# Two token blocks as one unit: first-layer matmuls of 256 rows in place of 128, and the weight traffic that goes with it

## The chip, the cores and the metric

The kernel runs on one core of a Trainium2 chip. The time is the device time of one execution in microseconds, the median of several runs. Five engines work side by side: TensorE (PE in the profile, its weight loads PEld), VectorE (DVE), ScalarE (ACT), GpSimd (POOL) and SyncE (SP), which issues nearly all transfers to 16 DMA engines. All arrays are 32-bit floats.

## The reference

Eight batches of 576 tokens go through a linear attention, a Fourier mix and a two-layer network:

```python
num = einsum('bhsm,bhmd->bhsd', phi(q), einsum('bhsm,bhsd->bhmd', phi(k), v))
x   = num / den                          # to (8, 576, 512)
u   = x + real(fft(fft(x, axis=1), axis=2))
un  = (u - mean(u)) / sqrt(var(u) + 1e-06)
out = u + maximum(un @ w_ch1, 0) @ w_ch2 # w_ch1 512 x 2048, w_ch2 2048 x 512
```

The change concerns the last line alone, and of the 4608 tokens in it those that go in blocks.

## The kernel before

**Two phases.** The first, up to about 421 us, does the attention, the Fourier mix and four plain rows of 128 tokens (`plain_of`, L1136), whose results `rest` (L1198) adds to u and stores. It ends in `listing.run` at L1415. The second (L1436) takes the other 4096 tokens in eight blocks of 512 (`NTB`, `TB`) and multiplies with two levels of Strassen-Winograd: a product of two matrices is cut into 2 x 2 parts and made of seven smaller products of sums of the parts, and each of these is cut again.

**First layer.** `first_of(j, i)` (L1466) makes outer product i (1 to 7) of block j. It consists of seven leaves (`leaf`, L1480), one for each inner product. A leaf is four matmuls, each with a stationary tile of 128 x 128 of a weight sum (left factor) and 128 rows (tokens) of a token sum: L1495. The rows are walked as 4 pieces of 32, a step that comes from the transposition in blocks of 32 (`by_blocks`, L1021). Each leaf's 128 x 512 result lies in a PSUM bank; VectorE and ScalarE copy it out, add it up (`save`, `added`, `moved`) and put it into four cells of `hid` (C11, C12, C21, C22). In block 0, products 2 to 7 are done with one level only (`single`, L1226), by matmuls of 256 rows at L1646.

**Weights of the first layer.** `w1` (128 x 4 x 2048) stays in SBUF, as do the outer sums `so[5]`, `so[6]`, `so[3]`, and `w1s`, the inner sums of product 1. Inner leaves 1, 2, 4 and 7 are read there in place. For the other products the inner sums 5, 6 and 3 are made once during block 0 (`w1_inner`, L1734), stored to DRAM (`w1l`, 18 stores of 256 KB) and loaded again for every block from 1 on, 18 loads a block (L1789).

**Second layer.** `product_of(j, i, cells)` (L1833) makes product i of block j: sums of hidden cells (`left_sums` L1687, `add_up` L1848), seven leaves of four matmuls (L1892) and the results' sums in `part` and `ur`. All its 49 weight tiles a block (`w2l`, 256 KB each) are loaded for every block (L1798). These and the first layer's loads share a ring of 12 buffers (`wl`, `NWL`).

**Tokens.** For block j, `norm_of` (L1061) loads 128 rows of u, normalizes them on ScalarE and POOL, transposes on VectorE (L1024) and stores to DRAM (`turned`, L1032). `fetched` (L1034) loads the tokens of half a block in four transfers of 128 KB (L1040). `block_norms` (L1270) then makes the outer token sums `tt` (L1290) and `token_sums` the inner ones (L1257), in `rx`.

**Order of the work.** Nothing is left to a scheduler: `manual_schedule` is on, and `Listing.run` (L233) merges generators of `Step`s into one order for each engine. A step names its engine, its planned time, what it waits for (`after`), the buffers it takes and gives, and a due time, which for block j, layer and product is

```python
    def due(j, layer, i):
        order_ = order(j) if layer else ORDER1 if j else ORDER0
        return LEAF * (98 * j + 49 * layer + 7 * order_.index(i))
```

The planner takes, among steps that can start at about the same time on an engine, the one due first. The start of the second phase is given instead by two strings, `PICKS2` and `BANKS2`. Transfers are planned with a rate (`Clock.rate`, 190 in `SECOND`, L56). At most three products are in flight (`set=3`). Transfers of all kinds stand in SP's one queue in the planned order, and a step that waits there holds back those behind it.

Of the kernel before, what the change touches and what calls it, by code (L numbers as in the profile page):

```python
# [1 line left out]

# [38 lines left out]
class Clock(NamedTuple):  # L41
# [14 lines left out]
SECOND = Clock(190.0, 0.15, 0.0, 0.1, {}, {}, (PE, ACT, DVE, POOL, SP, NONE), {})  # L56
# [41 lines left out]
    "0w0w0v000u0v0x0y0y0v0y0x0x0v0y0w0z0y0u0t1z0M0u0M1K0K0u1v0Q0N0I0t0W0M0O1L1w0L1U1t0S0Q0R0u010U0S0O0G0G"  # L98
    "0P0T1u0R0s0s000S0O0N0N0T0I0P0z0L0Q0R1R0B0K1P0P0K0K0T0V0I0S0G0U0T0S0U1s0H1r0D0z0x0A1N0w0F0S0P0F0E0O1O"
    "1u0R0v0G0V0V0V0C0S1S0R0L0w0P0S1r0V0M0Q0O0u0y0R0H0L1s0U0P0E0F0M0R1r0D0W0M0#0&0u0T0$0W0M0R0J0L0C0O0V00"  # L100
    "0$0N1q0M0R0G0A0V0u0Z0A0A0Z0R0U0D0S0S0L0G0Z0H0P1Y0F0F0Z0Y1q0$0$0C0D0D0U0T0X0T0#0X0z0V0F0U0V0X0C0B0W0P"
    "0R0U0T0U0v0T0x0Y0N1P0z0u0O0z0I0T0M0N0T0K0A0N0R0x0G0W1F0X0L0I0M0I0x0G0T0U0x0R0R0x0G0I0A0R0G0O0O0E0x0M"
    "0V0U000t0E1G1t0T1L0K0B0O0E0P1L0M0u0K0G1Q0L0R1z0N0C0E0G0E0u0G0D0L1D0N0C1Q0K1O0L0S0M0y0C0T0A0B1L0t0U0U"
    "0T0G0L0R0O0E0R0K0O0M0A0J0L0E1r1z1R0z0K0C0y0y0M0O0M1t0I0A0F0D0C0J0I0E1D0L0C0s1K0H0F0J0J0w0z0I0D0E0H1E"
    "0C0J1E0F0p0M0o0L1K1H1N0M0B0O0G0C0F0J0A0J0J0N0p1G0C1B0H0N0y0E0E0I1H0y1K0G0z0B0L0H0G0N1H0M0H0M0M0M0M1E"
    "0C1J0G0B1I0B1E0y0G0u1E0F0B0D1D1E0u0F0F0y0A0z0y0G0C0J0A0p0D0G0y1G0C0F0z0p0E0u1w0A0D1w0y0y0x0z0F0t0E0B"
    "0F0E1x1v1z1D0C0A0E0E0C0z0t1z0D0C0D1C0B0D0u0x0B0r0x0C0v0A1y0v0u0v0t0t0A0u0o0s0z0A1x0y0C0z0y0A0x0D0A0t"
    "0D0E0E0E0D0A0z0y0z0B0q0s0C0A0x1r0x0z0z1t1D1D0t0s0u0v0r0t0v000u0u0q0r0A1A0x0z0A0s0z0A1q0z0x0y0A0p0v0u"
    "0x0p0p0z0x0x0y0t0w0y0r0q0v0r0q000n0t0E0r0r0n0E0F0A0A0A0G0z0F0p0x0z0L0L0x0z0y0x0H0J0o0w0G0C0G0m0x0v0E"
    "0w0z0A0v0B0x0F0G0A0D0B0I0z0z0G0C0m0E0x0y"  # L110
)
BANKS2 = (
    "5670152675637645127567567560754361752071640532471365062476735"
# [219 lines left out]
def kernel(  # L333
# [10 lines left out]
    nc = tc.nc  # L344
# [42 lines left out]
    w1 = const.tile([128, NDC, DFF], F32, name="w1")  # L387
# [633 lines left out]
    def by_blocks(j, i, pool, u, h, k):  # L1021
        yield Step(DVE, 0.69, take=("turn",), give=("u",), makes=("turn", j, i))
        w = pool.tile([P, 4, NDC, Q], F32, name="turn", tag="turn", bufs=1)
        nc.vector.transpose(  # L1024
            out=w[:].rearrange("p g d q -> p d g q"),
            in_=u[:].rearrange("p (d g q) -> p d g q", d=NDC, g=4),
        )
        if (j, h) not in turned:
            turned[j, h] = dram.tile([P, 4, 2, NDC * Q], F32, name=f"turned{j}_{h}")
        t = turned[j, h]  # L1030
        yield Step(SP, 0.55, 6.0, after=(("turn", j, i),), makes=("turned", j, i), give=("turn",), kb=165)
        nc.sync.dma_start(t[:, :, k], w[:].rearrange("p g d q -> p g (d q)"))  # L1032

    def fetched(j, h, dst):  # L1034
        yield Step(
            SP, 1.7, 3.0, after=(("turned", j, 2 * h), ("turned", j, 2 * h + 1)),
            makes=("unT", j, h), kb=330,
        )
        for g in range(4):
            nc.sync.dma_start(  # L1040
                dst[Q * g : Q * g + Q].rearrange("q (b k) d t -> q b (k d t)", k=2),
                turned[j, h][:, g].rearrange("(b q) k n -> q b (k n)", q=Q),
            )

    def normed(j, pool):
        t0 = (NPLAIN * TP + TB * j) // 128

        def paced(i):
            h, k = divmod(i, HT // 128)
            yield Step(  # L1050
                NONE,
                after=events_of(range(t0, t0 + TB // 128)) + ((("first", j - 1, (1, 1, 5, 2)[i]), "y"),),
            )
            yield from norm_of(
                j, t0 + 2 * h, i, pool, None, (h, k), ((("first", j - 1, (6, 2, 7, 3)[i]), "y"),)
            )

        for i in range(TB // 128):
            yield Fork(paced(i), LEAF * (98 * j - 60 + 8 * i))

    def norm_of(j, t, i, pool, dst, block=None, after=()):  # L1061

        yield Step(SP, 0.42, 3.0, take=("u",), kb=256)
# [134 lines left out]
    def rest(t, b, yp):  # L1198
# [6 lines left out]
        store_rows(t, ur[:])  # L1205

# [18 lines left out]

    def single(j):  # L1226

        return () if j else ORDER0[1:]
# [10 lines left out]
    def tokens(j, i, n):  # L1239

        whole = outer_tokens(j, i)
        if n in (1, 2, 3, 7):
            t, d = {1: (0, 0), 2: (0, 1), 3: (1, 1), 7: (1, 0)}[n]
            return whole[:, 4 * t : 4 * t + 4, d]
        return extra_of(j, i)[:, (5, 6, 4).index(n)]

    def extra_of(j, i):
        if i == 1:
# [10 lines left out]
    def token_sums(j):  # L1259
        if j == 1:  # L1260
            yield Step(NONE, after=tuple(("w1l", i, n) for i in twice(1) for n in (5, 6, 3)))
        for i in twice(j):
            for m, op in enumerate(inner_tokens(j, i)):
                yield Step(
                    DVE, 0.28, after=(("tt", j),), makes=("tokens", j, i) if m == 3 else None, port=True,
# [4 lines left out]
    def block_norms(j, pool):  # L1270
        t0 = (NPLAIN * TP + TB * j) // 128
        yield Step(NONE, take=("slab",) * 4, after=events_of(range(t0, t0 + TB // 128)) + ("converted",))
# [36 lines left out]


# [63 lines left out]
    GW = F2 // 2  # L1374
    w1s = const.tile([128, 4, GW], F32, name="w1s")

# [7 lines left out]
    def weights_of(j, i, n):  # L1384
# [21 lines left out]
    def pairs(start):  # L1406
# [28 lines left out]
        slab=0, u=2, turn=1, ur=3, s=6, sq=5, set=3, wl=NWL, sums=NSUM, part=4,  # L1435
    ).items()}  # L1436
    hid = late.tile([128, 4, 2, 2, 4 * P], F32, name="hid")
    so.update({i: late.tile([128, D2, F2], F32, name=f"so{i}") for i in (5, 6, 3)})
# [7 lines left out]
    def cell_of(c, f, t):  # L1446
        return hid[:, c, f, t]
# [7 lines left out]
    def add(o, l, r, op, engines=(POOL, DVE), **kw):  # L1455
        n = math.prod(o.shape[1:]) / 512
        step = Step({e: {POOL: 1.3, DVE: 0.65}[e] * n + 0.05 for e in engines}, port=True, **kw)
# [8 lines left out]
    def first_of(j, i):  # L1466
        me = ("first", j, i)
        slot, read = slot_of(j, i), READ.get(i)
        free = ((("second", j - 1, read), "read"),) if read and j else ()
        merged, final = i in WITH, i in (2, 3, 4)  # L1470
# [3 lines left out]
        def over(f, t):  # L1474

            if i == 2:
                return (("h", j, 6, f, t),) if j else ()
            return {7: (("h", j, "u4", f, t),), 4: (("h", j, "sum", f, t),)}.get(i, ())

        def leaf(n, ps, start, after=(), take=(), give=(), makes=None):  # L1480
            own = n in (5, 6, 3) and i != 1
            w = ("wx", 1) if i == 1 else ("wx", j, i, n) if own else ("so", i, n)
            token = (("tokens", j, i),) if i != 1 else (("tt", j),)
            yield Step(
                PE, 0.895, after=token + (w,) + after, take=take, give=(("wl",) if own else ()) + give,
# [7 lines left out]
            left, right = weights_of(j, i, n), tokens(j, i, n)  # L1493
            for f in range(4):
                nc.tensor.matmul(  # L1495
                    ps[:, P * f : P * f + P].rearrange("f (b q) -> f b q", q=Q),
# [8 lines left out]
        def made(f, t):  # L1505
            return ("h", j, i, f, t)

        def with_(f, t):
            return (("h", j, BEFORE[i], f, t),)
# [48 lines left out]
        def last_cell(f, t):  # L1558
            o = cell_of(C22, f, t)
            after = ("h", j, 7, f, t), ("h", j, "u4", f, t)  # L1560
            yield from add(o, o, cell_of(C21, f, t), ALU.add, after=after, makes=("h", j, "sum", f, t), bias=due(j, 0, 4) - due(j, 0, 5) - 1)
# [3 lines left out]
        def u4_cell(f, t):  # L1565
# [3 lines left out]
                after=(read, made(f, t), ("h", j, 6, f, t)), makes=("h", j, "u4", f, t),  # L1569
# [10 lines left out]
        if i in single(j):  # L1580
# [19 lines left out]
            def u4_of(f, c, b, ps):  # L1600
                read = ((("second", j - 1, READ["u4"]), "read"),) if j else tuple(
                    ("h", j, n, f, t) for n in (2, 6) for t in range(2)
                )
                yield Step(
                    DVE, 0.7, 0.1, after=read + tuple(("h", j, 6, f, t) for t in range(2)) + ((me, "half", f, c),),
# [4 lines left out]
            def whole(f):  # L1610
# [4 lines left out]
                else:  # L1615
                    here = tuple(("h", j, "u4 half", f, c) for c in range(2))
                    for t in range(2):
                        yield Step(NONE, after=here, makes=("h", j, "u4", f, t))
# [69 lines left out]

# [382 lines left out]
```

## Time and profile before

| | |
|---|---|
| median of 3 runs | 1131.79 us (1131.77 to 1135.15) |
| profiled execution | 1134.51 us, span 1132.7 us |
| TensorE | busy 1116.3 us of the span |
| VectorE, ScalarE, POOL | busy 867.6, 541.7, 428.1 us |
| DMA | 258.30 MB, mean 228 GB/s |
| first-layer matmuls of 128 rows (L1495) | about 275 ns each from start to end, pipelined |
| one-level matmuls of 256 rows (L1646) | about 379 ns each, pipelined |
| w2 loads, first-layer weight loads | 392 and 126 of 256 KB |
| granted TensorE clock | 1.00 in nearly every stretch |

The span is what the profiler saw of one execution; the device time lies around it. "Busy" counts the time in which at least one instruction of an engine runs. Since matmuls overlap, the cost of one is not its mean duration but the distance to the next, read from a run of them without gaps. In the lines of the profile an instruction group is written as line, engine, operation, output<-input; an arrow before a name at the end tells what a wait ended with.

### The profile page before, as it was taken

What the parts mean: (1) busy time and instruction counts of PE and PEld (TensorE: products, weight loads), DVE (VectorE), ACT (ScalarE), POOL (GpSimd) and SP (SyncE); (2) the same over time, 40 slices, a digit from 0 to 9 for tenths busy, and PEclk for the clock granted to TensorE, in tenths of its full rate; (3) what the DMA queues carried; (4) which work ended last, traced back from release to release, by engine and by line L of the source; (5) the groups of instructions that cost most, each with busy time, mean ns of one, the idle gap of its engine ahead of it and who ended that gap; (6) DMA issues with size and microseconds to landing.
All of it is one profiled execution on the core that took longest, in us unless ns stands there. A gap on an engine that the chain in (4) does not pass through costs nothing.

```text
span 1132.7 us, 34265 instructions
## 1 busy us (share of the span) xinstructions
PE 1116.3 (99%) x13643; PEld 1040.2 (92%) x13643; DVE 867.6 (77%) x1732; ACT 541.7 (48%) x1644; POOL 428.1 (38%) x438
## 2 busy tenths in 40 slices
PE   8999999999999999999999999999999999999998
PEld 7778888879868778999999999999999999999998
DVE  6999899987576655796787778678678678678666
ACT  7888898856535216614424424424423522522311
POOL 2443443654573214613612710710720630540361
PEclk9999999999999999999999999999999999999999
DMA  7856766565763238797797798797698698798576
GB/s 242 224 177 180 224 181 215 170 206 170 222 196 126 93 92 284 211 314 246 227 339 232 219 329 241 213 326 258 202 323 264 210 281 298 214 268 293 184 223 205
DMA packets 187966, 258.30 MB, mean 228 GB/s; under 512 B 52384, under 2 KB 83360, under 8 KB 187808
## 3 DMA queue, kind: packets, MB, share of 16 engines
q1 hardware_dynamic: 187312, 255.85, 73.1%
q8 instruction: 109, 1.79, 0.7%
q14 instruction: 49, 0.40, 0.1%
q10 hardware_dynamic: 496, 0.26, 0.1%
HBM read 212.27 MB, written 47.97 MB: 230 GB/s over the span
## 4 chain that ended last, share of the span: by engine, by line
PE 89%; DVE 4%; ACT 3%; DMA 2%; issue 1%; SPq 0%; DVEq 0%; ACTq 0%
PE banks L1892 28%; PE banks L1495 28%; PE banks L1167 5%; PE banks L658 5%; PE banks L1190 5%; PE banks L564 4%; PE banks L1646 4%; PE banks L692 3%; PE banks L739 2%; PE banks L901 2%; ACT e L618 1%; PE banks L851 1%; DMA unT<-turned 1%; DVE nmx L601 1%; PE banks L861 1%
## 5 line engine op out<-in xcount | busy, mean ns | idle before, releaser
L1892 PE MATMUL banks<-wl,sums 128*128 128x128 f32 x1792 | 218.9, 275 | 0.7 <-DVE sums L1460 0.7
L1892 PEld LDWEIGHTS banks<-wl,sums 128*128 128x128 f32 x1792 | 209.3, 192 | 1.1 <-DVE sums L1460 0.9
L618 ACT ACTIVATE e<-banks,nmx 128x128 f32<-128x128 f32 x576 | 164.3, 423 | 24.3 <-DVE nmx L601 23.7
L1460 POOL TENSOR_TENSOR hid<-hid 128x512 f32<-128x512 f32 x97 | 127.0, 1314 | 119.1 <-ACT hid L1552 66.5
L1892 PE MATMUL banks<-wl,hid 128*128 128x128 f32 x1344 | 170.6, 275 | 0.6 <-DVE part L1870 0.4
L1892 PEld LDWEIGHTS banks<-wl,hid 128*128 128x128 f32 x1344 | 160.2, 192 | 1.1 <-DVE part L1870 0.6
L601 DVE TENSOR_REDUCE nmx<-banks 128x8 f32<-128x1024 f32 (+1 forms) x96 | 89.4, 952 | 18.3 <-PE banks L658 14.2
L1495 PE MATMUL banks<-rx,wx 128*128 128x128 f32 x672 | 88.8, 275 | 0.0
L1865 ACT ACTIVATE s<-banks 128x128 f32<-128x128 f32 x112 | 30.8, 277 | 113.2 <-PE banks L1892 97.7
L1495 PEld LDWEIGHTS banks<-rx,wx 128*128 128x128 f32 x672 | 81.8, 192 | 0.0
L658 PE MATMUL banks<-om,kqT 64*64 64x128 f32 (+1 forms) x2088 | 78.7, 275 | 2.2 <-ACT kv L708 1.9
L1538 DVE TENSOR_TENSOR hid<-banks,s 128x512 f32<-128x512 f32 x72 | 49.7, 691 | 38.9 <-PE banks L1495 36.9
L658 PEld LDWEIGHTS banks<-om,kqT 64*64 64x64 f32 (+1 forms) x2088 | 64.3, 138 | 13.1 <-issue 3.6
L1870 DVE TENSOR_TENSOR part<-banks,s 128x128 f32<-128x128 f32 x112 | 32.1, 288 | 50.0 <-PE banks L1892 48.8
L1520 ACT ACTIVATE s<-banks 128x512 f32<-128x512 f32 x65 | 38.7, 596 | 59.7 <-PE banks L1495 58.6
L1167 PE MATMUL banks<-unT,w 128*128 128x128 f32 x512 | 65.4, 279 | 1.7 <-DVE qeT L578 1.7
L507 POOL TENSOR_TENSOR w<-w,raw 128x512 f32<-128x512 f32 x28 | 37.7, 1356 | 77.6 <-DVE raw L501 77.6
L1442 DVE CUSTOM_DVE_ANT_0 hid<-banks,s 128x512 f32<-128x512 f32 x63 | 43.6, 692 | 27.5 <-PE banks L1495 25.2
L1167 PEld LDWEIGHTS banks<-unT,w 128*128 128x128 f32 x512 | 60.2, 192 | 4.5 <-issue 2.3
L1460 DVE TENSOR_TENSOR hid<-hid 128x512 f32<-128x512 f32 x91 | 61.1, 712 | 3.8 <-ACT hid L1598 3.8
L1518 DVE TENSOR_TENSOR s<-banks,hid 128x512 f32<-128x512 f32 x70 | 48.4, 691 | 19.0 <-PE banks L1495 16.7
L1941 POOL TENSOR_TENSOR ur<-ur,part 128x512 f32<-128x512 f32 x21 | 26.8, 1281 | 95.4 <-ACT part L1934 91.6
(200 smaller groups left out, 2387.4 us busy)
## 6 DMA issues: line engine op xcount, KB each, us to landing
wl<-w2l SPq DMA_DIRECT2D x392, 256.0 KB
wx<-w1l SPq DMA_DIRECT2D x126, 256.0 KB
raw<-in_moe_w_ch_dram SPq DMA_DIRECT2D x32, 512.0 KB
kq<-in_k_dram SPq DMA_DIRECT2D x32, 288.0 KB
kq<-in_q_dram SPq DMA_DIRECT2D x32, 288.0 KB
vd<-in_v_dram SPq DMA_DIRECT2D x32, 288.0 KB
u<-us SPq DMA_DIRECT2D x36, 256.0 KB
ur<-us SPq DMA_DIRECT2D x36, 256.0 KB
```

The costliest lines, as they stand in the source:

```text
L564: nc.tensor.transpose(ps[:, (j - j0) * 128 : (j - j0 + 1) * 128], src(j), ident[:])
L601: nc.vector.tensor_reduce(nmx[:, :, 0:num], pps[:, :, 0 : MF * num].rearrange("p b (c m) -> p b c m", m=MF), axis=AX.X, op=ALU.max, negate ...
L618: nc.scalar.activation(out=e[:, c + (i if num == 1 else 0), :], in_=pps[:, i, MF * c : MF * c + MF], func=AF.Exp, bias=nmx[:, i, c : c + 1],)
L658: nc.tensor.matmul(pps[cols, c, MF * m : MF * m + MF], lhsT=kqT[rows, j, cols], rhs=om2[rows, :],)
L1167: nc.tensor.matmul(hp[:, 0:TP], lhsT=w1[:, dc, 128 * fc : 128 * fc + 128], rhs=unTs[key][:, dc, :], start=(dc == 0), stop=(dc == NDC - 1),)
L1190: nc.tensor.matmul(yp[:, 0:DM], lhsT=hs[fc][:, 128 * i : 128 * i + 128], rhs=w2[:, fc, :], start=(fc == 0), stop=(fc == NFC - 1),)
L1460: eng.tensor_tensor(out=o, in0=l, in1=r, op=op)
L1495: nc.tensor.matmul(ps[:, P * f : P * f + P].rearrange("f (b q) -> f b q", q=Q), lhsT=left[:, P * f : P * f + P], rhs=right, start=start an ...
L1518: nc.vector.tensor_tensor(out=s[:], in0=ps, in1=cell_of(addend, f, t), op=ALU.add)
L1538: nc.vector.tensor_tensor(out=o, in0=ps, in1=kept[saved][:], op=ALU.add)
L1646: nc.tensor.matmul(cell.rearrange("f t (b q) -> f t b q", q=Q), lhsT=w[:, d, col : col + 128], rhs=right[:, :, d].rearrange("f (t b) q -> ...
L1892: nc.tensor.matmul(ps[:, 0:128], lhsT=left[:, f], rhs=wls[j, i, n][:, f], start=start and f == 0, stop=(f == 3), skip_group_check=True,)
```

## The change

From block 2 on, two blocks (2 and 3, 4 and 5, 6 and 7) form a unit (`WIDE`, `head`, `unit`, `passes`).

- First layer: a product is done in two passes g, each with half of the weight columns (256 of 512) and the tokens of both blocks. A leaf is two matmuls of 256 rows in place of four of 128. Cells hold both blocks' hidden values; half of them lie in `hid`, half in the memory of `w1` (`spread`, `widened`, `moved`).
- Because `w1` is given up, all 49 inner weight tiles are stored to DRAM (`w1x`): the 18 as before, nine that are plain parts of w1 right behind the stores of the first three plain rows (`RAW`, in `rest`), 12 during block 0, six during block 1 and four after the first pass of unit 2's product 1 (`w1_stored`). Units load them by two half tiles a transfer. Unit 2's product 1 reads w1 and `w1s` in place.
- Second layer: product i of the first block is followed by product i of the second with the same weight tile, which is loaded once for both.
- Tokens: both blocks of a unit are fetched before it, in twice as many transfers of 64 KB, into the memory of `so[5]` and `so[6]`; token sums are of 256 tokens; norms are paced over the unit before.
- The planner's transfer rate goes from 190 to 240, with new `PICKS2` and `BANKS2`; sums of hidden cells in the last unit go to VectorE only; the last order of products holds for both blocks of the last unit.

```diff
-SECOND = Clock(190.0, ...
+SECOND = Clock(240.0, ...
...
+        for i, n in RAW[4 * t : 4 * t + 4] if t < 3 else ():
+            nc.sync.dma_start(leaf_in(i, n), weights_of(0, i, n))
+    RAW = [(i, n) for i in (1, 2, 4) for n in (1, 2, 4)]
...
+    WIDE = 2
+    def wide(j):
+        return j >= WIDE
+    def head(j):
+        return j - (j - WIDE) % 2 if wide(j) else j
+    HEADS = tuple(j for j in range(NTB) if head(j) == j)
+    def unit(j):
+        return range(j, j + 2 if wide(j) else j + 1)
+    def passes(j):
+        return range(2 if wide(j) else 1)
...
-    def weights_of(j, i, n):
+    def weights_of(j, i, n, g=0):
+        if wide(j) and (j, i) == (WIDE, 1):
+            return weights_of(0, 1, n)[:, 256 * g : 256 * g + 256]
+        if wide(j):
+            m = PARTS.index(n) + 7 * g
+            return wxs[j, i, m // 2][:, m % 2]
...
-            left, right = weights_of(j, i, n), tokens(j, i, n)
-            for f in range(4):
+            left, right = weights_of(j, i, n, g), tokens(j, i, n)
+            for f in range(4 * P // span):
                 nc.tensor.matmul(
-                    ps[:, P * f : P * f + P].rearrange("f (b q) -> f b q", q=Q),
+                    ps[:, span * f : span * f + span].rearrange("f (b q) -> f b q", q=Q),
                     lhsT=left[:, P * f : P * f + P],
...
+        free += ("moved",) if (j, i) == (WIDE, ORDER1[1]) else ()
...
+    def w1_stored():
+        for k, (i, n) in enumerate((i, n) for i in (6, 5, 7, 3) for n in (1, 2, 4)):
+            after = tuple(("sum", i, d, f) for d in range(2) for f in range(2))
+            yield from w1_store(i, n, after, LEAF * (20 + 2 * k))
+        for k, i in enumerate(INNER):
+            yield from w1_store(i, 7, (("so", i, 7), (("first", 1, ORDER1[k], 0), "y")), LEAF * (102 + 7 * k))
+        for n in (5, 6, 3, 7):
+            yield from w1_store(1, n, ((("first", WIDE, 1, 0), "y"),), LEAF * 196)
...
+            for i in ORDER1[j == WIDE :] if wide(j) else ():
+                for m in range(7):
+                    after = tuple(("w1x", i, PARTS[k % 7]) for k in (2 * m, 2 * m + 1))
+                    yield Step(SP, 0.45, 2.6, take=("wl",), after=after, kb=165, makes=("wx", j, i, m),
+                               bias=due(j, 0, i) + LEAF * 2 * m - 14)
+                    wx = late.tile([128, 2, GW // 2], F32, name="wxw", tag="wl", bufs=NWL)
...
+    def widened():
+        yield Step(
+            NONE,
+            after=tuple(("w1x", 3, n) for n in PARTS) + tuple((("first", WIDE - 1, i, 0), "leaves") for i in ORDER1),
+        )
+        spread(hid[:].rearrange("p c f t n -> p (c f t n)"))
...
+    def moved():
+        yield Step(
+            NONE,
+            after=tuple(("w1x", i, n) for i in ORDER1 for n in PARTS)
+            + tuple((("first", WIDE, 1, g), "leaves") for g in range(2)),
+            makes="moved",
+        )
+        spread(const.tile([128, 4 * DFF], F32, name="hx", tag="w1")[:])
...
             for i in order(j):
-                yield Step(NONE, take=("set",))
-                yield Fork(product_of(j, i, cells), due(j, 1, i))
+                for k in unit(j):
+                    yield Step(NONE, take=("set",))
+                    yield Fork(product_of(k, i, cells[k]), due(k, 1, i))
```

## The prediction

> **What bounds the kernel now.** I read four views in this order: busy time per engine, TensorE's waits from the first block on, the chain that ended last in order of time, and busy time by stretches.
>
> ```profile
> PE 1116.3 (99%) x13643; PEld 1040.2 (92%) x13643; DVE 867.6 (77%) x1732; ACT 541.7 (48%) x1644; POOL 428.1 (38%) x438
> ```
>
> A busy share alone proves little, so next come TensorE's own waits between 400 and 1133 us (engine, line, what it waited for, us in total, times, longest).
>
> ```profile
> PE banks L1892 <- DVE sums L1460: 0.9, 2, 0.7
> PE banks L1892 <- DVE part L1870: 0.4, 1, 0.4
> ```
>
> In the last 733 us TensorE waits 1.3 us. So in the eight blocks the time is the number of matmuls times their period, and only a change of that period, or a new wait, can move it. The period is read from unbroken runs in the chain (start us, us, engine, line, instructions).
>
> ```profile
> 408.06 13.73 PE banks L1190 x32
> ...
> 432.15 32.81 PE banks L1646 x152
> ...
> 484.15 5.20 DMA unT<-turned
> 489.42 5.12 DMA wl<-w2l
> 494.55 7.66 DMA unT<-turned
> 505.85 1.68 DVE part L1941
> 508.39 2.94 PE banks L1892 x24
> ...
> 1046.30 36.63 PE banks L1495 x328
> 1084.71 1.79 PE banks L1892 x16
> 1087.39 40.21 PE banks L1892 x360
> ```
>
> Each fp32 matmul is recorded as two instructions. L1495, 128 rows: 36.63 / 328 = 111.68 ns a record. L1646, block 0's one-level products with 256 rows: 32.81 / 152 = 215.86 ns. L1190, 512 rows: 13.73 / 32 = 429.1 ns. L1892: 40.21 / 360 = 111.69 ns. The three DMA links at 484 to 502 us are the only place after the start where the chain leaves the engines: there block 1's tokens land just in time. The stretches show why (us; PE, PEld, DVE, ACT, POOL busy; clock, DMA share, GB/s).
>
> ```profile
> 440.00:450.00 10.00, 10.00 (x48) 8.81 (x47) 7.08 (x12) 7.84 (x19) 3.33 (x5) 1.00 0.83 276
> 450.00:460.00 10.00, 10.00 (x48) 8.81 (x47) 5.66 (x8) 7.99 (x15) 9.64 (x9) 1.00 0.62 190
> 460.00:470.00 10.00, 10.00 (x63) 9.20 (x63) 8.64 (x10) 9.00 (x19) 7.31 (x7) 1.00 0.62 162
> 470.00:480.00 10.00, 10.00 (x77) 9.59 (x76) 7.39 (x13) 4.65 (x13) 4.76 (x6) 1.00 0.86 277
> 480.00:490.00 10.00, 10.00 (x92) 10.00 (x91) 9.97 (x15) 2.06 (x9) 4.00 (x3) 1.00 1.01 274
> 490.00:500.00 10.00, 10.00 (x92) 10.00 (x91) 8.95 (x18) 1.92 (x8) 0.00 (x0) 1.00 1.08 325
> 500.00:510.00 10.00, 9.27 (x83) 9.08 (x82) 8.42 (x18) 1.43 (x6) 1.44 (x1) 1.00 1.01 342
> ```
>
> From 480 to 510 us the DMA engines are full, and that is where TensorE's 0.7 us wait falls. Before it, at 440 to 480, they have room. The clock is 1.00 throughout.
>
> **The change part by part.**
>
> *256 rows per instruction.* Blocks 2 to 7 hold 6 x 49 x 4 = 1176 first-layer matmuls of 128 rows, 2352 records, 2352 x 111.68 = 262.7 us. Three units need 588 of 256 rows, 1176 records, 1176 x 215.86 = 253.9 us. That is -8.8 us. L1646 has the same stationary tile and a token operand in the same pieces of 32, so I take its period. From below, at the 128-row period per row, the saving is 0; the other end is -8.8. All of it lies on the path, since TensorE has no gap to lose it in.
>
> [...]
>
> *Second layer in pairs.* The 98 products of a unit are as many as before, at 111.69 ns a record: 0 us. Weights of w2 are loaded once for two blocks, 49 loads of 256 KB in place of 98; the first layer loads 49 in place of 36 (42 in unit 2, whose first product reads w1). The unit moves 98 loads in place of 134, 9.4 MB less. In a narrow block the 49 w2 loads fall in 43.8 us (293 GB/s), now in 87.5. TensorE did not wait for them, so this gains 0; it removes a risk in units 2 to 6. If the 12 buffers ever ran dry, a late load would cost its lateness.
>
> *VectorE and ScalarE work.* Cell copies (0.69 us) and left sums (0.71) keep their number and size. Token sums halve in number and double in size: 56 x 0.285 = 16.0 us against 28 x 0.42 = 11.8 a unit (0.42 estimated on the line between 0.285 at 128 and 0.69 at 512 elements). In the last unit the left sums go to VectorE alone: about 16 that POOL might take, 11 us in 167. VectorE is busy about 68 of 91 us in a block; TensorE's queue covers both, 0 us. The least margin is in the first layer, where a leaf gets 0.863 us in place of 0.893 while a copy takes 0.69; other products stand between, as before. Without that cover each such copy would show up to its own 0.69 us.
>
> *Nine stores beside the plain rows.* They are put behind the row stores at about 303, 347 and 389 us on SP's queue, 256 KB each. SP spends about 0.4 us on one, at most 1.7 us for four, and behind them stand the loads of k, q, v and rows. DMA share between 340 and 400 us is 0.21 to 0.39 in slices of 20 us. I take 0; from above 3.3 us, if SP's 9 x 0.37 delayed the loads one for one; below nothing there is no gain, since nothing is taken out of that stage.
>
> *Twenty-two more stores and an earlier block 2.* Twelve stores (products 6, 5, 7, 3) and four u loads and four transposed stores of block 2 move into 440 to 480 us: 20 x 0.262 = 5.2 MB, at the 311 GB/s of the full stretch 16.9 us of DMA time. Room there is 10 x (0.17 + 0.38 + 0.38 + 0.14) = 10.7 us. So 6.2 us run over into the full stretch, ahead of block 1's tokens and block 0's w2 loads. These loads go out 12 leaves ahead (12 x 0.893 = 10.7 us) and land in 5.1 to 7.7 us by the chain, a lead of about 4.2 us. The wait becomes 6.2 - 4.2 = +2.0 us, in place and on top of the 0.7. Bounds: 0 (the stores slip into 405 to 430 us) and 6.2 (tokens have no lead, as the 0.7 us wait suggests). What is late next is VectorE: its sums for block 1 wait for the tokens, and block 0's part sums stand behind them. Six more stores and block 3's norms fall at 515 to 560 us (share 0.60 to 0.92), the tokens of both blocks at 560 to 600; the four stores of w1s wait for unit 2's first product, with only weight loads behind them on SP.
>
> *The same norms on ScalarE, POOL and VectorE.* Each of block 2's four brings three ScalarE passes of about 0.65 us, three small POOL operations and a transpose of 0.70. ScalarE gets 4 x 1.95 = 7.8 us more between 440 and 470, where it is busy 24.8 of 30 us copying block 0's PSUM tiles: 2.6 us too much, if nothing slips. But the stretch after it has 5.3 us free and block 2's tokens are wanted only at 600, so I take 0; from above 2.6 us, if PSUM copies queue behind a norm; no gain is possible there. On POOL's queue the norms stand among w1's sums (1.3 us each), and POOL is idle 9.7 of the 30 us.
>
> *Entry into unit 2.* Half of the hidden cells move into w1's memory, so product 6's first copy (and VectorE's queue behind it) waits until product 1 has read w1, two passes of 7 leaves. At worst it stands a whole pass, 7 x 0.863 = 6.0 us; at best the planned interleaving covers it, 0. The two passes and product 6 overlap, with three sets of copies in flight, so I take +0.5.
>
> *The end.* Block 6's last 512 KB now leave just before block 7's. At 311 GB/s they are 1.7 us; today the last small store issues at 1129.49 and the span ends at 1132.7. Bounds 0 and 1.7, I take +0.5.
>
> *Sum.* The profiled execution took 1134.51 us (span 1132.7 and 1.8 around it): 1134.51 - 8.8 + 2.0 + 0.5 + 0.5 = 1128.7. It is 2.7 above the median of the three runs (1131.79, from 1131.77 to 1135.15), so by the median 1131.79 - 5.8 = 1126.0 us.
>
> **The rivals.** 0.3% of 1131.79, 3.4 us, is about what a measurement of this kernel tells from no change: faster is below 1128.4, slower above 1135.2.
>
> *Slower: late loads in blocks 0 and 1.* Between 430 and 605 us the change adds 18 stores (4.7 MB) and, net, one block's u, transposed rows and tokens (3.1 MB): 7.8 MB, 25 us of DMA time. Room in that stretch, 1 - share summed over its slices of 10 us, is about 28 us, but not where it is needed. If none of it is found, the buffers' lead of 10.7 us is used up and 25 - 10.7 = 14.3 us of waits follow: 1131.79 - 8.8 + 14.3 = 1137.3. It decides from 12.2 us of waits. For it: the DMA share of 1.01 to 1.08 at 480 to 510 and of 1.05 and 1.04 at 570 to 590. Against: the early stores are spread, and 440 to 470 has room.
>
> *No difference: the entry.* A whole pass of 6.0 us is lost at unit 2, beside the 2.0 and 0.5 above: 1131.79 - 8.8 + 8.5 = 1131.5. For it: VectorE's other copies stand behind the waiting one. Against: product 6 is due 14 leaves after product 1 starts, when both passes are through.
>
> *Smaller saving.* On the line between the records of 128 and 512 rows (111.68 and 429.1 ns) one of 256 rows takes 217.5 ns; 1176 x (217.5 - 215.86) = 1.9 us come back: 1127.9, still faster. For it: L1646 ran in one stage only, with weights from w1 and its sums, and the new weights come from buffers that a DMA fills. Against: L1495's records are as long with either. [...]
>
> *All hidden.* No late loads, a covered entry, and the old 1.1 us of waits gone: 1131.79 - 9.9 = 1121.9. It is the forecast's lower end.
>
> **How the numbers follow.** The forecast with its own range of 1121.9 to 1128.4 gets 0.62: the saving is a measured row, and the additions' bounds are small against it. The smaller saving gets 0.05, the entry 0.13, the slower rival 0.20. So faster 0.62 + 0.05 = 0.67, same 0.13, slower 0.20. The range goes from 1121.5 over the entry's case to 1136.5, which leaves out most of the slower rival.
>
> **What would show it.** First-layer records of units 2 to 6 with 128x256 at 215.9 ns, 1176 of them, and no TensorE wait from 620 us on. A wait of 1 to 4 us at 480 to 515 with a DMA behind it, a DMA share of about 0.7 in the units, and 0 to 1 us of VectorE wait at unit 2's second product. Wrong it would be if TensorE waits more than 5.4 us in total after 420 us, or if the period is above 217 ns, or if TensorE's stretch up to 421 us grows by more than 1 us.

## The result and the profile after

The changed kernel takes 1141.74 us (median of 6 runs, 1139.35 to 1147.27), the kernel before on the same chip 1132.49 us: a ratio of 1.0081 with a 95% interval of 1.0053 to 1.011. It is slower, by 0.8%; 1126.0 was forecast, and the range ended at 1136.5. The profiled execution is the slowest of the six (1147.27 us) and has a span of 1145.5 us against 1132.7, 12.8 us more, where the medians differ by 9.2; what follows takes this one execution apart. Below, a difference between two kernels of different batches is the difference of their ratios times 1132.5 us.

First busy time, then TensorE's waits from 420 to 625 us, then lines of the chain that ended last (start us, us, what), the upper ones from 505 us on.

```profile
PE 1116.9 (98%) x12467; PEld 1006.4 (88%) x12467; DVE 881.9 (77%) x1703; ACT 541.4 (47%) x1644; POOL 358.3 (31%) x383
```

```profile
PE banks L2080 <- DMA wl<-w2l: 6.5, 6, 2.8
PE banks L2080 <- DVE hid L1567: 2.1, 1, 2.1
...
```

```profile
512.54 10.43 DMA u<-us
526.75 8.48 DMA u<-us
535.96 7.62 DMA u<-us
543.64 6.59 DMA u<-us
...
562.89 8.44 DMA u<-us
575.40 7.65 DMA wl<-w2l
...
623.58 81.17 PE banks L1638 x376
...
1055.97 83.98 PE banks L2080 x752
...
1140.33 1.17 PE banks L2080 x8
```

The same chain before, at block 2's first long run and at the end:

```profile
605.13 39.31 PE banks L1495 x352
...
1127.98 1.17 PE banks L1892 x8
```

The long runs from 623.58 and 1055.97 us are the part that came true: 81.17 / 376 = 215.88 ns for a record of 256 rows, 83.98 / 752 = 111.68 ns for one of 128. Three units are 3 x (392 x 215.88 + 784 x 111.68 ns) = 516.5 us, six single blocks were 525.3.

The upper lines are the loss. Counted back from the start of the last run of records (1140.33 us after, 1127.98 before), less the three units or six blocks and 2.9 and 0.6 us of waits in them, block 2's work starts at about 620.9 us instead of 602.1: 18.8 us later. Its first long run starts 18.45 us later (623.58 and 605.13). Block 0 starts at the same time (423.47 and 423.34 us). So the whole loss lies in blocks 0 and 1, nearly all of it from 520 us on, in block 1: between 420 and 515 us TensorE waits 0.24 us. There the chain no longer runs through TensorE but through loads of u, the rows that the norms of blocks 2 and 3 wait for. TensorE's waits to 625 us come to 10.2 us. The stretches show a second loss (us; PE, PEld, DVE, ACT, POOL busy; clock, DMA share, GB/s):

```profile
560.00:570.00 10.00, 9.96 (x71) 9.62 (x72) 8.12 (x13) 3.49 (x10) 3.38 (x5) 0.83 0.92 233
...
580.00:590.00 10.00, 7.23 (x42) 7.07 (x42) 3.04 (x7) 2.95 (x8) 2.17 (x4) 0.66 0.94 283
...
610.00:620.00 10.00, 8.47 (x54) 7.82 (x53) 5.29 (x10) 1.95 (x6) 0.00 (x0) 0.83 1.03 347
```

The granted clock falls to 0.83, 0.66 and 0.83 in the mean of these stretches, which is 10 x (0.17 + 0.34 + 0.17) = 6.8 us of full-speed work. In stretches of 1 us it is 0.50 for 3.4 us from 561, for 6.8 us from 582 and for 3.4 us from 612 us, and 1.00 between. Eight records of 128 rows took 2.05 us from start to end at 0.50 (from 583.19 us) and 1.06 at 1.00 (from 592.03). 1.6 us of the slow time lie in a wait, where half speed costs nothing more, so the clock adds 6.8 - 0.8 = 6.0 us. 10.2 + 6.0 = 16.2 of the 18.8 us; the other 2.6 are not assigned. With the 18.8 us the span's terms are 18.8 - 8.8 + 2.3 (waits inside the units) + 0.45 (the end) = 12.75. That this meets the 12.8 is no check of its own, since the 18.8 was counted back with the same terms.

What occupies block 1 is seen in the view of the tile u between 505 and 605 us: the transposition that ends each norm, of the kernel before and of the changed one (duration ns min/median/max, first and last start).

```profile
L1024 DVE STREAM_TRANSPOSE turn<-u x4: 702/702/704, 529.9 to 567.1; 128x512 f32<-128x512 f32 x4
```

```profile
L1030 DVE STREAM_TRANSPOSE turn<-u x8: 696/707/712, 525.4 to 589.8; 128x512 f32<-128x512 f32 x8
```

Eight norms in place of four, one after another until 590 us, into block 1's second layer. ScalarE's own waits from 505 to 625 us say what each of them waited for:

```profile
ACT junk L1107 <- DMA u<-us: 21.2, 8, 6.8
```

Before, that wait was 1.4 us, once. What the DMA engines move is not what grew where the time was lost: from 560 to 625 us their share is 0.89 in both kernels, at 279 GB/s before and 265 after; from 505 to 560 us it went from 0.75 to 0.87.

### The profile page after: what moved, and what is told of

Same layout as the page of the kernel before. It is cut to its first block, busy times and chain, and to the rows that moved or that the text cites. A ratio compares the mean times of both kernels' runs of the same rounds, so it can differ in the third digit from the quotient of the medians.

```text
span 1145.5 us, 31511 instructions
## 1 busy us (share of the span) xinstructions
PE 1116.9 (98%) x12467; PEld 1006.4 (88%) x12467; DVE 881.9 (77%) x1703; ACT 541.4 (47%) x1644; POOL 358.3 (31%) x383
## 4 chain that ended last, share of the span: by engine, by line
PE 81%; DMA 10%; DVE 3%; ACT 3%; issue 1%; SPq 0%; POOL 0%; DVEq 0%; ACTq 0%; POOLq 0%
PE banks L2080 28%; PE banks L1638 22%; DMA u<-us 5%; PE banks L1198 5%; PE banks L1221 4%; PE banks L563 4%; PE banks L657 4%; PE banks L1789 4%; PE banks L691 2%; DMA wl<-w2l 2%; PE banks L738 2%; PE banks L900 2%; PE banks L850 1%; ACT e L617 1%; DMA raw<-in_moe_w_ch_dram 1%
## 5 line engine op out<-in xcount | busy, mean ns | idle before, releaser
L2080 PE MATMUL banks<-wl,hid 128*128 128x128 f32 x768 | 101.2, 278 | 8.8 <-DMA wl<-w2l 6.1
L2080 PEld LDWEIGHTS banks<-wl,hid 128*128 128x128 f32 x768 | 93.9, 194 | 10.5 <-issue 4.8
L1638 PE MATMUL banks<-unw,wxw 128*128 128x256 f32 x352 | 85.0, 379 | 0.9 <-DVE s L1661 0.9
L2080 PE MATMUL banks<-wl,hx 128*128 128x128 f32 x576 | 74.3, 276 | 2.0 <-ACT banks L2096 1.6
L1638 PEld LDWEIGHTS banks<-unw,wxw 128*128 128x128 f32 x352 | 66.5, 190 | 10.1 <-DVE s L1661 1.3
L2080 PEld LDWEIGHTS banks<-wl,hx 128*128 128x128 f32 x576 | 69.4, 192 | 2.8 <-ACT banks L2096 2.0
L1638 PE MATMUL banks<-rx,wxw 128*128 128x256 f32 x288 | 71.0, 379 | 0.0
L1638 PE MATMUL banks<-ttw,wxw 128*128 128x256 f32 x288 | 69.7, 379 | 0.0
L1638 PEld LDWEIGHTS banks<-ttw,wxw 128*128 128x128 f32 x288 | 54.5, 190 | 7.6 <-DVE s L1661 0.2
L1638 PEld LDWEIGHTS banks<-rx,wxw 128*128 128x128 f32 x288 | 54.5, 190 | 7.3
```

Of the source, the lines that this page charges most:

```text
L1638: nc.tensor.matmul(ps[:, span * f : span * f + span].rearrange("f (b q) -> f b q", q=Q), lhsT=left[:, P * f : P * f + P], rhs=right, start ...
L2080: nc.tensor.matmul(ps[:, 0:128], lhsT=left[:, f], rhs=wls[head(j), i, n][:, f], start=start and f == 0, stop=(f == 3), skip_group_check=True,)
```

## The experiments

In the expectations, theory U is that the u loads land late because of their shape, V that the added bytes, the stores of weight sums above all, are too many for block 1, W that SP's one queue holds weight loads behind waiting steps, C that the single `turn` buffer makes a chain.

### u loads in another shape

The load's DRAM side is four pieces of 32 rows (`k b q d`). This run issues four transfers of 32 rows instead; the next does the same to the kernel before.

```diff
-            nc.sync.dma_start(u[:], rows[block[1]])
+            for b in range(4):
+                nc.sync.dma_start(u[Q * b : Q * b + Q, :], rows[block[1]][b])
```

> The changed kernel, but each late load of 128 rows of u is issued as four transfers of 32 rows; the bytes, their order and all else stay. [...] Theory V (the bytes of stores, tokens and weights together are too many for block 1): nothing changes but SP's three more issues a load; 1139 to 1145. Theory W (SP waits for each norm's transposed rows, whatever the load takes): 1136 to 1142.

Measured: 1136.39 us, ratio 1.0033 (1.0012 to 1.0054), 5.4 us less than the change as it is. ScalarE's wait for u, and TensorE's for weights from 420 to 625 us:

```profile
ACT junk L1108 <- DMA u<-us: 5.2, 3, 3.4
```

```profile
PE banks L2081 <- DMA wl<-w2l: 7.0, 6, 4.0
```

ScalarE's wait falls from 21.2 to 5.2 us and the u loads leave the chain, but TensorE still waits as long for weights, and the ratio is still above 1. The shape is one cause, not the only one.

> The kernel before with the same cut of the late u loads into four transfers. TensorE waited 1.3 us in all in its blocks, so by every theory the time stays within 1.5 us of the kernel before; by theory U the DMA share at 480 to 510 us falls a little below the 1.01 to 1.08 seen.

Measured: 1133.16 us, ratio 1.0004 (0.9988 to 1.002). Where four norms stand in a block, the shape of their loads costs nothing.

### The added stores alone

The kernel before with 21 of the 31 stores of weight sums, nine beside the plain rows and twelve in block 0:

```diff
         nc.sync.dma_start(w1l[i][(5, 6, 3).index(n)], w)
+        if i in (6, 5, 7, 3):
+            nc.sync.dma_start(w1x[i][(5, 6, 3).index(n)], weights_of(0, i, (1, 2, 4)[(5, 6, 3).index(n)]))
...
         store_rows(t, ur[:])
+        for i, n in RAW[4 * t : 4 * t + 4] if t < 3 else ():
+            nc.sync.dma_start(w1x[i][(1, 2, 4).index(n)], weights_of(0, i, n))
```

> The kernel before with 21 of the 31 added stores alone: the nine behind the stores of the first three plain rows, and twelve of products 6, 5, 7 and 3 during block 0, each right behind one of the stores that are there. Nothing reads them. Theory V (store bytes): TensorE waits of 3 to 6 us at 480 to 560 us and 3 to 7 us in the time. Theories U and W: 0 to 2 us.

Measured: 1133.56 us, ratio 1.0007 (0.9994 to 1.0019). Theory V falls for these 21 stores. The other ten were not tried by themselves; all 31 are in the run with the work alone, below, which shows no loss.

### Block 3's norms: none, transfers alone, engine work alone

Three cuts of the four norms that the change brings into block 1. In the first they are left out, and only their steps stay in the plan (block 3 then reads block 2's tokens); in the second the u load and the turned store stay and the work between them goes; in the third the work stays, on a constant buffer, and both transfers go. None of the three computes block 3's part of the output: it is made of other tokens, or of rows that are not normalized. The second also changes a wait, since its store reads the u buffer itself and holds it until it has landed. The edit of the first:

```diff
     def norm_of(j, t, i, pool, dst, block=None, after=()):
+        if block and j == 3:
+            for s in steps:
+                yield s
+            return
```

> The changed kernel without block 3's four norms: their u loads, ScalarE, POOL and VectorE work and stores of transposed rows are left out, and block 3 takes the transposed rows of block 2 for its tokens, so its part of the output is that of other tokens. Transfers that fetch tokens stay. Theories U and W (eight norms in one block instead of four): the waits between 420 and 625 us fall below 4 us and the time by 8 to 15 us, to 1127 to 1134. Theory V: by the 2 MB that fall away, 0 to 4 us.

> The changed kernel with block 3's four norms kept as transfers only: each u load and each store of 256 KB of transposed rows stays in its place, but the store takes the loaded rows as they are; the ScalarE, POOL and VectorE work of these norms is left out, so block 3's output is wrong. If the norms cost by their transfers (landing, queue places, bytes): 1138 to 1143, as the changed kernel. If by the chain of work between load and store and by its engine time: 1127 to 1131, as without the norms.

> The counterpart: block 3's four norms with their ScalarE, POOL and VectorE work (on a constant tile in place of loaded rows) but without the u loads and without the stores of transposed rows; block 3 takes block 2's transposed rows, so its output is wrong. Transfers to blame: 1127 to 1131. Engine work to blame: 1138 to 1143.

Measured: without them 1128.62 us, ratio 0.9967 (0.9952 to 0.9981); transfers alone 1146.32, 1.0137 (1.0103 to 1.017); work alone 1126.2, 0.9951 (0.9933 to 0.997). TensorE's waits for weights, 420 to 625 us, with transfers alone and with work alone:

```profile
PE banks L2098 <- DMA wl<-w2l: 13.4, 7, 5.5
```

```profile
PE banks L2115 <- DMA wl<-w2l: 0.5, 1, 0.5
```

This is the central result: (1.0081 - 0.9951) x 1132.5 = 14.7 us hang on four u loads and four turned stores, 2 MB, and nothing on the norms' engine work. Without these eight transfers the kernel takes the time that was forecast; that it does so within 0.2 us is luck, since the forecast counts them and has 2.0 us of waits that did not come. The stretch from 560 to 625 us, of the change as it is and of the run with the work alone:

```profile
560.00:625.00 65.00, 57.81 (x428) 55.48 (x429) 42.19 (x75) 18.56 (x55) 12.89 (x17) 0.89 0.89 265
```

```profile
560.00:625.00 65.00, 64.28 (x467) 60.84 (x467) 53.48 (x96) 25.55 (x66) 14.74 (x19) 1.00 0.88 277
```

With the work alone the DMA engines are as busy and move more in this stretch, and TensorE neither waits nor loses its clock.

### Other queues, another buffer

If waiting steps in SP's queue held the weight loads back, moving such steps to POOL's queue should help. Moved were the 96 token transfers of `fetched`, then the turned stores, then both with the u loads.

```diff
-                    nc.sync.dma_start(
+                    nc.gpsimd.dma_start(
                         dst[Q * g : Q * g + Q, t].rearrange("q (b k) d x -> q b (k d x)", k=2),
...
-        nc.sync.dma_start(t[:, :, k], w.rearrange("p g d q -> p g (d q)"))
+        (nc.gpsimd if wide(j) else nc.sync).dma_start(t[:, :, k], w.rearrange("p g d q -> p g (d q)"))
```

> The changed kernel with the 96 token transfers of the units (64 KB each) issued by POOL's queue in place of SP's; bytes and waits stay. If SP's queue is what is short (32 issues of 0.43 us between weight loads, and waits that stand in front of them): TensorE's waits for weight loads between 550 and 625 us fall by more than half and the time to 1129 to 1136. If the DMA engines or the u loads' landing are what is short: 1138 to 1144.

> The changed kernel with the units' stores of transposed rows issued by POOL's queue in place of SP's, so that SP no longer waits there for ScalarE, POOL and VectorE to finish a norm. If SP's waiting for a norm holds the weight loads (theory W): 1128 to 1136. If the u loads' landing itself is the trouble (theory U): 1137 to 1143, since a u load's buffer still comes free only after the norm.

> The changed kernel with all steps of the units' norm chain (u loads, stores of transposed rows, token transfers) issued by POOL's queue, so that SP holds weight loads, stores of results and w1 stores alone. If weight loads are late because SP's queue stands behind the chain: TensorE's waits for weight loads fall below 2 us, a wait for tokens at unit 2's start stays (up to 10 us), 1130 to 1138. If the transfers themselves are slow: 1140 to 1146.

Measured: 1144.79 us, ratio 1.0112 (1.0083 to 1.0142); 1144.38, 1.0108 (1.008 to 1.0136); 1151.91, 1.0147 (1.0122 to 1.0172). None is faster than the change. In the last, TensorE waits only 0.3 us for weights from 505 to 630 us (3.2 from 420 on), in place of 6.2, as theory W has it; but waits for ScalarE and VectorE take their place (3.1 for a PSUM bank, 1.7 for `part`), and its chain then runs through POOL's steps and the turned stores. So the sign of theory W came and its time did not. POOL's own costs are mixed in (from 505 to 625 us the token transfers' steps on POOL are 11.3% of that chain), and W stays open.

A second turn buffer, in the constant buffer `ur1`, for every other norm; then the same with the u loads of the first experiment and truer landing times in the plan:

```diff
-        more = j > WIDE + 1 and i % 2
+        more = wide(j) and i % 2
...
+            w = ur1[:].rearrange("p (g d q) -> p g d q", g=4, d=NDC)
```

> The changed kernel with a second buffer for transposed rows: in every unit the odd norms transpose into the tile ur1, which is free after the plain rows, in place of the one turn buffer (the planner is told so). All work stays. Theory C (the eight norms of unit 2 are a chain: a transposition waits until the store before it has landed, 7 to 9 us, and SP's and ScalarE's queues stand behind it, so the weight loads come late): the norms of unit 2 end before 580 us instead of 595, TensorE's waits between 420 and 625 us fall from 10 us to 2 to 5, and the time to 1128 to 1134. Theory D (the DMA engines have too much to move there): 1139 to 1144, as the changed kernel.

> The same second buffer, and each late load of u cut into four transfers of 32 rows, the planner being told of 1.5 us of SP and 6 us to landing for them in place of 0.42 and 9. Theory C: both waits of the chain are shorter, the norms end before 575 us, no clock loss, and 1124 to 1129, faster than the kernel before by some 5 us. Theory D: 1134 to 1140, as with the cut loads alone.

Measured: 1148.26 us, ratio 1.0124 (1.0103 to 1.0146), and 1137.48, 1.0033 (1.0014 to 1.0052). Alone, the buffer makes the change no faster (the median is 4.9 us above it); with the new loads the ratio is that of the new loads alone. Theory C falls.

### Bytes, loads, stores

All of block 3's norm steps stay where they are, but with a quarter of the bytes: in both transfers, in the u loads alone, in the turned stores alone. Block 3's part of the output is then made of other rows.

```diff
+            if j == 3:
+                nc.sync.dma_start(u[:, 0:128], rows[block[1]][:, :, 0:128])
...
+        if j == 3:
+            nc.sync.dma_start(t[:, 0:1, k], w.rearrange("p g d q -> p g (d q)")[:, 0:1])
```

> The changed kernel with a quarter of the bytes in block 3's four u loads (128 of 512 columns, in the same four pieces) and in its four turned stores (128 of 512 pieces of 512 B); all steps, queues, waits and engine passes stay, and the passes take their values from other rows, so block 3's part of the output is of other tokens. 1.5 MB less in block 1. If the loss goes with the bytes (capacity): three quarters of the 15 us between the changed kernel and the one without these transfers come back, about 1130. If it goes with the number of transfers and their places in the queue: 1139 to 1142, no change.

> As the one before, but only the u loads are cut to a quarter; the turned stores are whole. [...] By capacity alone: half of the gain, about 1136. By the theory of the stores' 512-byte pieces: no gain, 1140 to 1142.

> Only block 3's four turned stores are cut to a quarter (128 of 512 pieces of 512 B each); its u loads are whole, and block 3 reads block 2's tokens. By late u loads: no gain, 1140 to 1142. By capacity alone: half, about 1136. By the stores' pieces: 1130 to 1133.

Measured: 1135.53 us, ratio 1.0014 (1.0 to 1.0029); 1135.11, 1.0013 (0.9998 to 1.0027); 1140.62, 1.0063 (1.0044 to 1.0082). Small loads win 7.7 us, small stores 2.0, which their intervals hardly tell from nothing, both together no more than the loads alone. So bytes as such are not it (both together save the most bytes and no more time), the u loads' size is half of it, and 14.7 - 7.6 = 7 us stay although 1.5 of the 2 MB are gone. With small stores and whole loads ScalarE waits as before:

```profile
ACT junk L1110 <- DMA u<-us: 20.9, 8, 7.0
```

### Units from block 4 on

Is it the crowd in block 1, or does entering a unit cost wherever it begins? `WIDE` becomes 4, with the old order of block 0; the 18 stores (each behind a product of block 1 or 2, `past`) and eight norms for the first unit are spread over the blocks before it, the norms over block 2's second layer and block 3's first. In this run product 4 of a second layer can overtake the last ReLU in front of it, so the last 128 rows of block 3 come out wrong; in the two runs after it, it waits.

```diff
-    WIDE = 2
+    WIDE = 4
...
-            yield from w1_store(i, n, after, LEAF * (20 + 2 * k))
+            yield from w1_store(i, n, after + (past[k][0],), LEAF * past[k][1])
```

> Units from block 4 on in place of block 2 (two units of two blocks); blocks 0 to 3 are single as before the change, with the old order of block 0. The 18 stores of weight sums are spread over blocks 1 and 2, one a product, and block 4's and 5's eight norms over block 2's second layer and block 3's first, one every 11 us or so. The saving of 256-row instructions is two thirds, 784 x 215.86 - 1568 x 111.68 = -5.9 us. If the loss of the changed kernel is the crowd of transfers in block 1 and not the units themselves: 1126 to 1129, faster than before. If units cost at their entry wherever they begin: 1134 to 1140.

Measured: 1153.98 us, ratio 1.0169 (1.0146 to 1.0192). Lines of its chain:

```profile
608.17 39.31 PE banks L1641 x352
653.14 10.14 DMA unT<-turned
664.53 8.37 DMA u<-us
672.97 6.27 DMA wl<-w2l
...
714.07 33.07 PE banks L1641 x296
```

The first layers (L1641) run nearly unbroken; the DMA links stand beside second layers. So in the next run every added store and norm was put beside a first layer, and in the one after it the u loads were cut as well.

> Units from block 4 on, as in the run before, but every added transfer is put beside a first layer of blocks 1, 2 and 3: six stores of weight sums and (in blocks 2 and 3) six norms in each, none beside a second layer. Also, product 4 of a second layer now waits for the last ReLU in front of it (in the run before it could overtake that, and the last 128 rows of block 3 came out wrong). The single blocks' second layers load 49 tiles of 256 KB in 43.8 us, 293 GB/s; the run before had all its waits there and none beside first layers. If that stage is what has no room: no wait above 3 us from 510 on and the saving of 5.9 us, 1126 to 1129. If units cost at their entry, or added transfers cost wherever they stand: 1134 or more.

> The run before with u loads as four transfers of 32 rows. If the late landing of u is a cause beside the place: 1 to 5 us below the run before. If the place decides alone: the same time, 1126 to 1129.

Measured: 1150.8 us, ratio 1.0131 (1.0108 to 1.0154), and 1139.73, 1.0054 (1.0037 to 1.007). Neither beats the kernel before. Again a line or two of each chain:

```profile
635.42 7.94 DMA u<-us
645.55 7.54 DMA u<-us
656.66 31.43 PE banks L2087 x264
```

```profile
742.85 4.68 DMA wl<-w2l
748.75 6.12 DMA wl<-w2l
```

With whole loads the six norms of block 2 did not stay beside its first layer: the u loads stand in the chain until 653 us, past its end. Cutting the loads alone wins (1.0131 - 1.0054) x 1132.5 = 8.7 us, more than in block 1. What is left is lost mainly at the last single block's second layer, 743 to 773 us, where both blocks' tokens are fetched: the entry costs there too.

### Bare stores beside first and second layers

Is a second layer simply full? In the kernel before, first and second layers alternate like this (block 1's second, block 2's first):

```profile
558.00:604.00 46.00, 46.00 (x415) 46.00 (x414) 37.16 (x74) 11.01 (x37) 8.41 (x10) 1.00 0.96 305
604.00:647.00 43.00, 43.00 (x388) 43.00 (x387) 29.82 (x56) 21.07 (x43) 23.53 (x26) 1.00 0.70 215
```

```diff
+        at = [(("first", j, i), "y") for j in (2, 3) for i in ORDER1]
+        at += [(("second", j, i), "p1") for j in (5, 6) for i in order(j)]
+        for k, e in enumerate(at):
+            yield Step(SP, 0.45, after=(e,))
+            nc.sync.dma_start(dram.tile([P, DM], F32, name=f"more{k}")[:], ur1[:])
```

> The kernel before with 28 plain stores of 256 KB from a constant buffer, that nothing reads and nothing waits for: one for each product beside the first layers of blocks 2 and 3, and one for each product beside the second layers of blocks 5 and 6. In the kernel before, DMA share and rate are 0.70 to 0.77 at 219 GB/s beside first layers and 0.95 to 0.99 at 305 GB/s beside second layers, without a wait of TensorE. If the second layer is full and the first is not: no wait between 603 and 735 us, and beside the two second layers 7 x 0.262 = 1.8 MB each, 6.0 us at 305 GB/s less 1 to 2 us of room, 4 to 5 us of waits for weights each, with TensorE's clock perhaps falling behind them: 1140 to 1146. If further transfers are hidden wherever they stand, as the 21 stores of an earlier run were: 1132 to 1135.

Measured: 1140.49 us, ratio 1.0058 (1.0041 to 1.0076). The first layer of block 2 and the second layers of blocks 5 and 6, with their extra stores:

```profile
603.00:647.00 44.00, 43.97 (x394) 43.77 (x394) 30.27 (x63) 21.25 (x44) 20.43 (x23) 1.00 0.81 263
...
911.00:958.00 47.00, 45.54 (x406) 45.21 (x405) 36.36 (x69) 11.22 (x37) 8.77 (x10) 1.00 1.03 331
...
1002.00:1050.00 48.00, 46.74 (x416) 46.42 (x415) 37.41 (x74) 12.55 (x39) 7.25 (x9) 1.00 1.01 329
```

By the chain's long runs against those of the kernel before, 1.8 MB beside a first layer cost 0.3 and 0.0 us, beside a second layer 1.2 and 1.8 us. The second layers are indeed the tight stage, but the price is 0.7 to 1.0 us a megabyte, a third of what was expected, and the clock stays at 1.00. That the time lies in the first case's range is therefore not that case's doing: in the profiled execution 2.9 us were gone before the first extra store, half of them before block 0, and what took them is not known. At this price of plain stores the change's extra 2 MB of norms and 1 MB of tokens beside block 1 would cost about 3 us, not 14.7.

## Why the prediction was wrong, point by point

- **256 rows per instruction, -8.8 us.** Right: 215.88 ns a record, against 215.86 taken from block 0.
- **Second layer in pairs, 0.** Right: 111.68 ns a record, and no wait for weights after 625 us.
- **VectorE and ScalarE work, 0.** Small miss: the units wait 1.6 us for ScalarE's PSUM copies, 0.9 and 0.4 for VectorE; before it was 0.6 from block 2 on.
- **Nine stores beside the plain rows, 0.** Right: block 0 starts 0.13 us later, and the experiment with the added stores alone measured no change.
- **Twenty-two more stores and an earlier block 2, +2.0.** This step failed, in two places. It assumed that block 2's norms move to 440 to 480 us. They did not: the first of the unit's u loads goes out at 511.87 us, and the +2.0 us of waits there did not come (0.24 between 420 and 515). And it put block 3's norms into "515 to 560 us (share 0.60 to 0.92)" in half a sentence, at no price. Eight norms then stood in block 1 and ran until 590 us, and TensorE lost 16.2 us there in waits and clock; the runs show 14.7 us for the transfers of block 3's four. The stores in this step were harmless: all of them are in the run of 1126.2 us. What was wrong in kind, and not only in size, is that transfers were priced by bytes over rate. A norm is a chain (load, three ScalarE passes with POOL between, transposition, store) with two u buffers and one turn buffer, on engines that do their steps in the planned order. What such a chain costs is argued here to be how late each load lands and who stands behind the wait; the runs show the first part (5 to 8 us) and leave the second open.
- **The same norms on ScalarE, POOL and VectorE, 0.** Right as engine work (1126.2 us with the work alone). But busy time was the wrong thing to look at: ScalarE was not too busy, it stood 21.2 us in front of late loads, with PSUM copies behind in its queue: after the longest wait, 6.8 us to 562.19 us, it did the norm's first two passes and then, from 563.67 us and without idle time, a PSUM copy.
- **Entry into unit 2, +0.5; the end, +0.5.** The first long run of the unit begins unbroken, and TensorE has no wait for `moved` in it; the end costs 5.17 us after the last run in place of 4.72, that is 0.45.
- **The rivals.** The slower one, late loads in blocks 0 and 1, was right in place and sign, and at 0.20 it was given too little. It priced 14.3 us of waits; there were 10.2, and 6.0 us of clock that no case had. That its 1137.3 us is the nearest figure is in part luck: its reason, bytes without room, is not what the runs show. The entry and the smaller saving did not happen.
- **The sign of being wrong.** It was set at more than 5.4 us of waits after 420 us. There were 10.2 + 2.9 = 13.1.

What is shown: the loss hangs on the eight transfers of block 3's norms (14.7 us), not on engine work, weight stores or the turn buffer; the u loads, by their shape or their size, are 5 to 8 us of it. What stays open: the other 7 us or so. At the price of the bare stores, bytes explain 3 at most. That the chain's waits in SP's and ScalarE's queues make the rest fits the run with work alone, and the run with the whole chain on POOL's queue in its weight waits (0.3 us), but in no time that was measured. Bringing block 2's norms into block 0, as the prediction assumed, was not tried, and why the plan left them in block 1 is open. No version that beats both kernels and computes everything was found; the nearest is the change with cut u loads, at 1.0033.

## What to carry to other kernels

When a change brings work forward, find for every step of it the time at which it will really run, and price a chain of dependent transfers by its landing time, its buffers and the queues that stand behind each wait, not by bytes over rate. Look for the fullest stage that it can slip into: here the loads that were planned beside a first layer at a DMA share of 0.7 ended beside a second layer at 0.96. And when a chain waits for a load like this one (256 KB as one transfer of four pieces), try it in more transfers early: it took two lines here, won 5.4 and 8.7 us, and cost nothing where nobody waited.

## What the runs showed of the hardware that was not expected

- **The clock falls at short waits.** In the changed kernel the longest single wait of TensorE in block 1 is 2.8 us, and the granted clock is 0.50 for 3.4, 6.8 and 3.4 us; that adds three fifths again to the waits (6.0 on 10.2 us). The longest waits at the three falls are 2.1, 2.8 and 1.5 us, and the second fall begins inside its wait. The length of a wait alone does not decide, since with the token transfers on POOL's queue a wait of 2.7 us at 577 us left the clock at 1.00. With waits of at most 0.8 us each (the bare stores) it stayed at 1.00.
- **The shape of a load.** Whole, a u load of 256 KB stands in the chain of block 1 for 6.6 to 8.5 us, and for 10.4 where two go out together; as four transfers of 64 KB each piece lands in a median of 3.6 us after its own issue, and the four issues of a load take 2.0 to 3.7 us. That is worth 5.4 us of kernel time in block 1 and 8.7 with units from block 4 on. Why the pieces land sooner is not shown: the trace does not tell which DMA engines one transfer used.
- **A full stage is not a wall.** At a DMA share of 0.96 and 305 GB/s TensorE waits for nothing, and 1.8 MB more raise the rate to 329 and 331 GB/s and cost 1.2 to 1.8 us.
